# Fused attention and two-layer product on one core: norms a pair later, second products moved between batches, weights in four transfers

The chip is one Trainium2 chip, of which one core runs the kernel. The metric is device time in microseconds of that core, as the median of several executions. "Span" is the length of the one profiled execution of a kernel, 1.7 to 2.0 us less than the timed figure of that same execution. In the profiles PE is TensorE, the matrix engine (PEld its weight loads), DVE is VectorE, ACT is ScalarE, POOL is GpSimd, and SP issues most transfers; L129 is line 129 of that kernel (the lines of the two kernels differ). The granted clock is the share of its full clock that the profile shows TensorE as having been given.

## What the kernel computes

```python
# q, k, v: (8 batches, 12 heads, 448 rows, 64)   w_in: (768, 2048)   w_out: (2048, 768)
q_n = q / (norm(q) + 1e-6);  k_n = k / (norm(k) + 1e-6)
attn = softmax(q_n @ k_n.T / tau)                    # per head
x = (attn @ v) with heads side by side               # 3584 x 768
h = x @ w_in
out = (h * clip(h + 3, 0, 6) / 6) @ w_out            # float32
```

The kernel treats two heads at a time: six pairs make a batch, 48 pairs in all. Scores can't overflow (the inputs are unit vectors), so the exponential takes no maximum first. While the attention of one batch runs, the two products of an earlier batch are fed to TensorE piece by piece as filling: this is "the stream". A unit of the first product is 6 matmuls of 448 columns, followed by a relu on ACT and a multiplication on DVE; a unit of the second product is 16 matmuls of 384 columns, followed by one copy and an out transfer.

## The kernel before

Cuts are marked.

```python
def square(i, eng):                       # cut: eng None splits it over ACT and DVE (pair 0 only)
    sq = sb.tile([128, 2, 7, D], FP32, name="sq", tag="sq", bufs=2)
    eng.tensor_tensor(out=sq[:, :, :, :], in0=a, in1=a, op=ALU.mult)

def norms(i):
    nc.vector.tensor_reduce(out=n2[:, :], in_=sq..., axis=AX.X, op=ALU.add)      # L129, DVE
    nc.scalar.activation(out=ln[:, :], in_=n2[:, :], func=AF.Ln)                 # L132, ACT
    nc.scalar.activation(out=nr[:, :], in_=ln[:, :], func=AF.Exp, scale=0.5)
    nc.scalar.activation(out=le[:, :], in_=nr[:, :], func=AF.Ln, bias=eps_bias[:, :])
    nc.scalar.activation(out=r[:, :], in_=le[:, :], func=AF.Exp, scale=-1.0)     # L135

def add_batch(b):                         # called when batch b's attention is done
    first = [mm1_unit(b, fc) for fc in range(FCN)] if b < B else []
    second = []
    if b > 0:
        p = b - 1
        second = [mm2_unit(p, t, m) for t in range(3 + p % 2) for m in range(2)]
    # cut: appends first to the stream with second spread evenly between

for i in range(NP):                       # a pair; four steps s, each one group of scores
    for s in range(4):
        # cut: at the third step of a batch's first pair: add_batch(i // HP - 1)
        scores(i, s, SC2 if i < HP and s % 2 else SC)      # matmuls, then exponential on ACT
        if s == 0:
            # cut: every second pair issues the loads of a later group of two pairs
            if i + 3 < NP:
                square(i + 3, nc.gpsimd)
            if i + 2 < NP:
                normalise(i + 2, nc.gpsimd)
                vcast(i + 2, nc.gpsimd)
            next_weights()                                 # one of eight transfers
            fill(0.6 * ns)
            if i > 0:
                values(i - 1, 3)
                finish_values(i - 1)                       # reciprocal and scaling on DVE
            fill(0.4 * ns)
        elif s == 1:
            fill(0.8 * ns)
            if i > 0:
                back(i - 1)                                # transposes back, copy to xT on DVE
            if i + 3 < NP:
                norms(i + 3)
            fill(0.2 * ns)
        elif s == 2:
            fill(0.4 * ns)
            if i + 1 < NP:
                transposes(i + 1)
            fill(0.6 * ns)
            values(i, 0)
            values(i, 1)
        else:
            fill(ns)
            values(i, 2)
```

A `norms` call stands in ACT's queue between two exponentials, and in the traces everything behind it there waits as long as it waits: from pair 12 to pair 42 ACT stood 54.4 us in 30 waits, 1.8 us each, at the first instruction of `norms`, with the next exponential behind it.

## Time and profile before

| | before |
|---|---|
| timed median | 510.05 us |
| span of the profiled run | 509.7 us |
| first exponential starts | 17.39 us |
| mark of pair 5 (end of the first batch) | 52.33 us |
| length between marks of pairs 6 and 12 | 56.85 us |
| sum of the next five such stretches | 283.5 us |
| ACT idle until a DVE reduction | 86.8 us |

"Mark" means the start of the reciprocal that closes a pair on DVE; there is one per pair, so marks date the parts of a run. The lines these figures come from are in the prediction. The profiled execution was itself timed at 511.44 us, 1.4 above the median.

### The profile page before, as it was taken

What the parts mean: (1) busy time and instruction counts of PE and PEld (TensorE: products, weight loads), DVE (VectorE), ACT (ScalarE), POOL (GpSimd) and SP (SyncE); (2) the same over time, 40 slices, a digit from 0 to 9 for tenths busy, and PEclk for the clock granted to TensorE, in tenths of its full rate; (3) what the DMA queues carried; (4) which work ended last, traced back from release to release, by engine and by line L of the source; (5) the groups of instructions that cost most, each with busy time, mean ns of one, the idle gap of its engine ahead of it and who ended that gap; (6) DMA issues with size and microseconds to landing.
All of it is one profiled execution on the core that took longest, in us unless ns stands there. A gap on an engine that the chain in (4) does not pass through costs nothing.

```text
span 509.7 us, 9679 instructions
## 1 busy us (share of the span) xinstructions
PE 449.6 (88%) x3872; PEld 274.9 (54%) x3872; DVE 259.3 (51%) x568; ACT 282.5 (55%) x543; POOL 189.3 (37%) x156
## 2 busy tenths in 40 slices
PE   0666767779999999999999999999999999999996
PEld 0343434445555656655555656655555656655563
DVE  5665545554645555554645555545645454433310
ACT  3566646666566655566566655566565655533300
POOL 2996275444344343344354343344353320000000
PEclk9988989999999999999999999999999999999999
DMA  7999994210432504514432505514431000010022
GB/s 211 251 221 221 239 221 110 68 41 17 125 97 60 140 15 140 140 39 120 125 90 66 141 18 139 141 36 120 125 107 50 32 27 21 32 48 32 31 78 63
DMA packets 71581, 50.96 MB, mean 100 GB/s; under 512 B 22384, under 2 KB 71536, under 8 KB 71536
## 3 DMA queue, kind: packets, MB, share of 16 engines
q1 hardware_dynamic: 65168, 43.53, 31.5%
q0 software_dynamic: 5248, 6.29, 7.0%
q8 instruction: 30, 0.49, 0.4%
q10 hardware_dynamic: 1120, 0.52, 0.4%
q14 instruction: 15, 0.12, 0.1%
HBM read 45.61 MB, written 11.01 MB: 111 GB/s over the span
## 4 chain that ended last, share of the span: by engine, by line
PE 60%; ACT 15%; DVE 10%; DMA 7%; SPq 4%; issue 2%; POOL 1%; ACTq 0%; POOLq 0%
PE M L286 17%; PE M L257 13%; PE SC L184 9%; PE Y L286 8%; ACT at L188 7%; PE Y L257 7%; DVE n L129 6%; DMA raw<-in_q_dram 5%; PE PV L214 4%; ACT le L134 2%; DVE xT L241 2%; PE Z L240 2%; SPq L95 1%; ACT u L267 1%; ACT nr L133 1%
## 5 line engine op out<-in xcount | busy, mean ns | idle before, releaser
L188 ACT ACTIVATE at<-SC 128x896 bf16<-128x896 f32 x192 | 156.4, 820 | 65.2 <-PE SC L184 63.7
L141 POOL TENSOR_TENSOR nrm<-raw,r 128x896 bf16<-128x896 f32 x46 | 77.6, 1687 | 206.9 <-ACT r L135 196.5
L184 PE MATMUL SC<-qT,kz 128*128 128x448 bf16 x336 | 97.9, 363 | 29.7 <-ACT at L188 28.4
L257 PE MATMUL M<-xT,w_in_sb 128*128 128x448 bf16 x510 | 120.8, 353 | 0.0
L286 PE MATMUL M<-w_out_sb,gT 128*128 128x384 bf16 x608 | 118.1, 326 | 0.0
L286 PEld LDWEIGHTS <-gT 128*128 128x128 bf16 x896 | 84.5, 98 | 60.2 <-issue 5.2
L257 PEld LDWEIGHTS <-w_in_sb 128*128 128x128 bf16 x768 | 72.5, 98 | 77.3 <-issue 22.1
L270 DVE SCALAR_TENSOR_TENSOR gT<-u,M 128x448 bf16<-128x448 bf16 x85 | 52.7, 621 | 98.3 <-ACT u L267 97.9
L119 POOL TENSOR_TENSOR sq<-raw 128x896 f32<-128x896 f32 x46 | 77.3, 1680 | 18.7 <-DMA raw<-in_q_dram 12.2
L214 PEld LDWEIGHTS <-at 128*128 128x128 bf16 x1344 | 64.0, 99 | 30.8 <-ACT at L188 9.3
L214 PE MATMUL PV<-vx,at 128*128 128x65 bf16 (+1 forms) x1344 | 71.7, 199 | 7.0 <-ACT at L188 6.9
L267 ACT ACTIVATE u<-M,half_bias 128x448 bf16<-128x448 f32 x85 | 53.4, 630 | 22.6 <-PE M L257 22.3
L257 PE MATMUL Y<-xT,w_in_sb 128*128 128x448 bf16 x258 | 63.1, 355 | 0.0
L132 ACT ACTIVATE ln<-n 128x14 f32<-128x14 f32 x48 | 10.3, 215 | 86.8 <-DVE n L129 86.8
L286 PE MATMUL Y<-w_out_sb,gT 128*128 128x384 bf16 x288 | 56.7, 326 | 0.0
L129 DVE TENSOR_REDUCE n<-sq 128x14 f32<-128x896 f32 x48 | 51.6, 1076 | 6.7 <-POOL sq L119 4.5
L270 DVE SCALAR_TENSOR_TENSOR gT<-u,Y 128x448 bf16<-128x448 bf16 x43 | 26.7, 621 | 46.3 <-ACT u L267 45.9
L184 PEld LDWEIGHTS <-kz 128*128 128x128 bf16 x336 | 29.7, 99 | 21.3 <-issue 7.9
L154 PE MATMUL Z<-ident,nrm 128*128 128x128 bf16 x336 | 27.9, 225 | 13.4 <-DVE nrm L141 11.4
L154 PEld LDWEIGHTS <-nrm 128*128 128x128 bf16 x336 | 23.9, 101 | 23.5 <-DVE nrm L141 11.4
L229 DVE TENSOR_TENSOR on<-PV,rc 128x512 bf16<-128x512 f32 x48 | 33.2, 691 | 1.7
L241 DVE COPY xT<-Z 128x448 bf16<-128x448 bf16 x48 | 18.7, 389 | 29.1 <-PE Z L240 29.1
(44 smaller groups left out, 244.7 us busy)
## 6 DMA issues: line engine op xcount, KB each, us to landing
out_dram<-o SPq DMA_DIRECT2D x48, 192.0 KB, 1.9
raw<-in_q_dram SPq DMA_DIRECT2D x23, 384.0 KB, 5.1
raw<-in_k_dram SPq DMA_DIRECT2D x23, 384.0 KB, 5.2
vr<-in_v_dram SPq DMA_DIRECT2D x23, 384.0 KB, 5.5
w_in_sb<-in_moe_w_in_dram POOLq DMA_DIRECT2D x4, 768.0 KB, 11.7
w_out_sb<-in_moe_w_out_dram POOLq DMA_DIRECT2D x4, 768.0 KB, 12.2
out_dram<-o SPq DMA_DIRECT2D x16, 96.0 KB, 2.2
raw<-in_q_dram SPq DMA_DIRECT2D x23, 64.0 KB, 4.8
```

Source lines behind the costliest of these rows:

```text
L119: eng.tensor_tensor(out=sq[:, :, :, :], in0=a, in1=a, op=ALU.mult)
L129: nc.vector.tensor_reduce(out=n2[:, :], in_=sq[:, :, :, :].rearrange("p h s d -> p (h s) d"), axis=AX.X, op=ALU.add)
L141: eng.tensor_tensor(out=nrm[:, :, :, :].rearrange("p s h d -> p h s d"), in0=raw_pair(i), in1=r_of[i][:, :].rearrange("p (h s) -> p h s", ...
L154: nc.tensor.transpose(Z[:, s * 128 : (s + 1) * 128], nrm[:, s, :, :], ident[:, :])
L184: nc.tensor.matmul(sc[:, n, 0:S], k_block(i, name), qT_of[i][:, :], start=True, stop=True)
L188: nc.scalar.activation(out=at[:, 0:m, :], in_=sc[:, 0:m, 0:S], func=AF.Exp, scale=inv_tau)
L214: nc.tensor.matmul(o, at[:, n, q_cols(i // HP, j)], mv, start=(name == "A0" and j % 2 == 0), stop=last, skip_group_check=True,)
L229: nc.vector.tensor_tensor(out=on[:, :, :, :].rearrange("p (b j) h d -> p b (j h) d", b=2), in0=pv4[:, :, :, 0:D], in1=rc[:, :, :].to_broad ...
L257: nc.tensor.matmul(ps[:, 0:S], w_in_sb[:, cc, fc * 128 : (fc + 1) * 128], x[:, cc, c0 : c0 + S], start=(cc == 0), stop=(cc == CC - 1),)
L267: nc.scalar.activation(out=u[:, :], in_=ps[:, 0:S], func=AF.Relu, bias=half_bias[:, :], scale=1.0 / 6.0)
L270: nc.vector.scalar_tensor_tensor(out=g[:, fc, c0 : c0 + S], in0=u[:, :], scalar=1.0, in1=ps[:, 0:S], op0=ALU.min, op1=ALU.mult,)
L286: nc.tensor.matmul(ps[:, 0:MH], lhs, w_out_sb[:, fc, m * MH : (m + 1) * MH], start=(fc == 0), stop=(fc == FCN - 1),)
```

## The change

Its intent is to fill TensorE earlier and to keep other engines from holding it up. The core of the diff; renamings and the untouched parts of the moved functions are cut.

```diff
+    def square(i, n_act, eng):          # ACT squares the first n_act of 7 slices, eng the rest
+    def reduce(i):                      # the DVE reduction, taken out of norms
...
     def add_batch(b):
-        second = [mm2_unit(p, t, m) ...]      # of the batch before, p = b - 1
+        first = [mm1_unit(b, fc) for fc in range(FCN)]
+        for n, u in enumerate(first):
+            stream.append(u)
+            if lagging and n % 3 == 2:
+                stream.append(lagging.pop(0))
+        second = [mm2_unit(b, t, m) for t in range(3 + b % 2) for m in range(2)]
+        n = len(second) - (LAG if 0 < b < B - 1 else 0)      # LAG = 4
+        stream.extend(second[:n])
+        lagging.extend(second[n:])
...
-    nc.scalar.preload_act_table_set(...)      # the second one
-    load(1); load(2)
+    load_qk(1); load_v(0); load_qk(2); load_v(1); load_v(2)
...      # eight weight transfers become four, at the start and at pairs 0, 3 and 5
-    square(0, None); norms(0); square(1, nc.vector); normalise(0, nc.vector); vcast(0, nc.gpsimd)
-    norms(1); transposes(0); normalise(1, nc.vector); square(2, nc.gpsimd); vcast(1, nc.gpsimd)
-    next_weights(); norms(2)
+    square(0, 3, nc.vector); reduce(0); norms(0); square(1, 4, nc.gpsimd); reduce(1)
+    normalise(0, nc.vector); transposes(0); norms(1); vcast(0, nc.gpsimd)
+    square(2, 4, nc.gpsimd); normalise(1, nc.gpsimd); vcast(1, nc.gpsimd)
+    next_weights(); reduce(2)
...
             if s == 0:
-                square(i + 3, nc.gpsimd); normalise(i + 2, nc.gpsimd); vcast(i + 2, nc.gpsimd)
             elif s == 1:
+                norms(i + 2)
                 fill(0.8 * ns)
                 back(i - 1)
-                norms(i + 3)
             elif s == 2:
+                square(i + 3, 3 if i < HP else 0, nc.gpsimd)
+                normalise(i + 2, nc.gpsimd); vcast(i + 2, nc.gpsimd)
             else:
+                reduce(i + 3)
```

More of the change, by code (lines that the diff above doesn't have):

```diff
@@ L74, with load_qk @@
     moe_banks = [Y]
-    raw_of, nrm_of, r_of, qT_of, at_of, on_of = {}, {}, {}, {}, {}, {}
-    def load(d, n_pairs=2, first=0, engs=None):
+    raw_of, sq_of, n2_of, nrm_of, r_of, qT_of, at_of, on_of = {}, {}, {}, {}, {}, {}, {}, {}
+    def load_qk(d, first=0, n_pairs=2, e0=nc.sync, e1=nc.sync):
         b, h = 2 * d // HP, 4 * d % H + 2 * first
@@ L84, in load @@
         raw = raw_of[d][:, 2 * first : 2 * (first + n_pairs), :, :]
-        vt = vr[d % NV][:, 2 * first : 2 * (first + n_pairs), :, :]
         hs = slice(h, h + 2 * n_pairs)
-        e0, e1 = engs or (nc.sync, nc.sync)
-        def main(t):
-            return t[b, hs, 0:SM, :].rearrange("h (p c) d -> p h c d", c=3)
         for n, t in enumerate((k, q) if b % 2 else (q, k)):
-            e0.dma_start(out=raw[:, :, 4 * n : 4 * n + 3, :], in_=main(t))
+            e0.dma_start(
+                out=raw[:, :, 4 * n : 4 * n + 3, :],
+                in_=t[b, hs, 0:SM, :].rearrange("h (p c) d -> p h c d", c=3),
+            )
             e1.dma_start(
@@ L98, in load, with load_v @@
             )
-        e1.dma_start(out=vt[:, :, 0:3, :], in_=main(v))
+    def load_v(d):
+        b, h = 2 * d // HP, 4 * d % H
+        vt, vs = vr[d % NV], v[b, h : h + 4]
+        nc.sync.dma_start(
+            out=vt[:, :, 0:3, :], in_=vs[:, 0:SM, :].rearrange("h (p c) d -> p h c d", c=3)
+        )
         for g in range(2):
-            e0.dma_start(
-                out=vt[64 * g : 64 * g + 64, :, 3, :].rearrange("p (i g) d -> p i g d", g=2)[:, :, g, :],
-                in_=v[b, hs, SM:S, :].rearrange("(i g) p d -> p i g d", g=2)[:, :, g, :],
+            nc.sync.dma_start(
+                out=vt[64 * g : 64 * g + 64, g:4:2, 3, :],
+                in_=vs[g:4:2, SM:S, :].rearrange("h p d -> p h d"),
             )
@@ L107, in raw_pair @@
         return raw_of[i // 2][:, 2 * (i % 2) : 2 * (i % 2) + 2, :, :]
-    def square(i, eng):
+    def square(i, n_act, eng):
         sq = sb.tile([128, 2, 7, D], FP32, name="sq", tag="sq", bufs=2)
-        r_of[i] = sq
+        sq_of[i] = sq
         a = raw_pair(i)
-        if eng is None:
-            nc.scalar.activation(out=sq[:, :, 0:3, :], in_=a[:, :, 0:3, :], func=AF.Square)
-            nc.vector.tensor_tensor(
-                out=sq[:, :, 3:7, :], in0=a[:, :, 3:7, :], in1=a[:, :, 3:7, :], op=ALU.mult
-            )
-        else:
-            eng.tensor_tensor(out=sq[:, :, :, :], in0=a, in1=a, op=ALU.mult)
+        if n_act:
+            nc.scalar.activation(
+                out=sq[:, :, 0:n_act, :], in_=a[:, :, 0:n_act, :], func=AF.Square
+            )
+        if n_act < 7:
+            eng.tensor_tensor(
+                out=sq[:, :, n_act:7, :], in0=a[:, :, n_act:7, :], in1=a[:, :, n_act:7, :], op=ALU.mult
+            )
+    def reduce(i):
+        n2 = sb.tile([128, 14], FP32, name="n2", tag="n2", bufs=3)
+        n2_of[i] = n2
+        nc.vector.tensor_reduce(
+            out=n2[:, :],
+            in_=sq_of.pop(i)[:, :, :, :].rearrange("p h s d -> p (h s) d"),
+            axis=AX.X,
+            op=ALU.add,
+        )
     def norms(i):
-        sq = r_of[i]
-        n2 = sb.tile([128, 14], FP32, name="n2", tag="n2", bufs=2)
+        n2 = n2_of.pop(i)
         ln = sb.tile([128, 14], FP32, name="ln", tag="ln", bufs=2)
@@ L128, in norms @@
         r = sb.tile([128, 14], FP32, name="r", tag="r", bufs=3)
-        nc.vector.tensor_reduce(
-            out=n2[:, :], in_=sq[:, :, :, :].rearrange("p h s d -> p (h s) d"), axis=AX.X, op=ALU.add
-        )
         nc.scalar.activation(out=ln[:, :], in_=n2[:, :], func=AF.Ln)
@@ L321, in fill @@
             stream_ns[0] -= step
+    LAG = 4
+    lagging = []
     def add_batch(b):
-        first = [mm1_unit(b, fc) for fc in range(FCN)] if b < B else []
-        second = []
-        if b > 0:
-            p = b - 1
-            second = [mm2_unit(p, t, m) for t in range(3 + p % 2) for m in range(2)]
-        stream_ns[0] += len(first) * CC * MM1_NS + len(second) * FCN * MM2_NS
-        done = 0
+        first = [mm1_unit(b, fc) for fc in range(FCN)]
         for n, u in enumerate(first):
             stream.append(u)
-            while second and done * len(first) < (n + 1) * (6 + 2 * ((b - 1) % 2)) - len(first):
-                stream.append(second.pop(0))
-                done += 1
-        stream.extend(second)
+            if lagging and n % 3 == 2:
+                stream.append(lagging.pop(0))
+                stream_ns[0] += FCN * MM2_NS
+        second = [mm2_unit(b, t, m) for t in range(3 + b % 2) for m in range(2)]
+        n = len(second) - (LAG if 0 < b < B - 1 else 0)
+        stream.extend(second[:n])
+        lagging.extend(second[n:])
+        stream_ns[0] += FCN * CC * MM1_NS + n * FCN * MM2_NS
     for t in vr:
@@ L342 @@
         nc.vector.memset(t[0:64, 1:4:2, 3, :], 0.0)
-    load(0, 1, 0, (nc.sync, nc.scalar))
-    load(0, 1, 1, (nc.sync, nc.scalar))
-    nc.scalar.preload_act_table_set("natural_log_exp_and_others")
-    load(1)
-    load(2)
+    load_qk(0, 0, 1, nc.sync, nc.scalar)
+    load_qk(0, 1, 1, nc.sync, nc.scalar)
+    load_qk(1)
+    load_v(0)
+    load_qk(2)
+    load_v(1)
+    load_v(2)
     nc.vector.memset(eps_bias, EPS)
@@ L350 @@
     make_identity(nc, ident)
-    nc.gpsimd.memset(kz[0][:, :, :], 0.0)
     for t in vx:
@@ L356 @@
         nc.vector.memset(t[64:128, 1, 3, D : D + 1], 1.0)
-    nc.gpsimd.memset(kz[1][:, :, :], 0.0)
-    FG = d_ff // 4
-    weights = [
-        (w_in_sb[:, :, f * FG : (f + 1) * FG], w_in_r[:, :, f * FG : (f + 1) * FG]) for f in range(4)
-    ] + [(w_out_sb[:, 4 * f : 4 * f + 4, :], w_out_r[:, 4 * f : 4 * f + 4, :]) for f in range(4)]
+    for t in kz:
+        nc.gpsimd.memset(t[:, :, :], 0.0)
+    weights = []
+    for f in range(2):
+        c = slice(f * d_ff // 2, (f + 1) * d_ff // 2)
+        weights.append((w_in_sb[:, :, c], w_in_r[:, :, c]))
+    for f in range(2):
+        c = slice(f * FCN // 2, (f + 1) * FCN // 2)
+        weights.append((w_out_sb[:, c, :], w_out_r[:, c, :]))
     def next_weights():
-        if weights:
-            o, w = weights.pop(0)
-            nc.gpsimd.dma_start(out=o, in_=w)
-    square(0, None)
+        o, w = weights.pop(0)
+        nc.gpsimd.dma_start(out=o, in_=w)
+    square(0, 3, nc.vector)
+    reduce(0)
     norms(0)
-    square(1, nc.vector)
+    square(1, 4, nc.gpsimd)
+    reduce(1)
     normalise(0, nc.vector)
+    transposes(0)
+    norms(1)
     vcast(0, nc.gpsimd)
-    norms(1)
-    transposes(0)
-    normalise(1, nc.vector)
-    square(2, nc.gpsimd)
+    square(2, 4, nc.gpsimd)
+    normalise(1, nc.gpsimd)
     vcast(1, nc.gpsimd)
     next_weights()
-    norms(2)
+    reduce(2)
     startup = ExitStack()
@@ L405 @@
                 if i % 2 and (i + 5) // 2 < NP // 2:
-                    load((i + 5) // 2)
-                if i + 3 < NP:
-                    square(i + 3, nc.gpsimd)
-                if i + 2 < NP:
-                    normalise(i + 2, nc.gpsimd)
-                    vcast(i + 2, nc.gpsimd)
-                next_weights()
+                    load_qk((i + 5) // 2)
+                    load_v((i + 5) // 2)
                 fill(0.6 * ns)
@@ L418 @@
             elif s == 1:
+                if i + 2 < NP:
+                    norms(i + 2)
                 fill(0.8 * ns)
@@ L421 @@
                     back(i - 1)
-                if i + 3 < NP:
-                    norms(i + 3)
                 fill(0.2 * ns)
             elif s == 2:
+                if i + 3 < NP:
+                    square(i + 3, 3 if i < HP else 0, nc.gpsimd)
+                if i + 2 < NP:
+                    normalise(i + 2, nc.gpsimd)
+                    vcast(i + 2, nc.gpsimd)
+                if i in (0, 3, 5):
+                    next_weights()
                 fill(0.4 * ns)
@@ L432 @@
             else:
+                if i + 3 < NP:
+                    reduce(i + 3)
                 fill(ns)
@@ L440 @@
     add_batch(B - 1)
-    add_batch(B)
     fill(1e9)
```

## The prediction

> **What bounds the kernel now.** I read the page's busy table and slices first, then stretches of time cut at the batches of heads, then who waits for whom, then the start instruction by instruction.
>
> ```profile
> PE   0666767779999999999999999999999999999996
> DMA  7999994210432504514432505514431000010022
> L129 DVE TENSOR_REDUCE n<-sq 128x14 f32<-128x896 f32 x48 | 51.6, 1076 | 6.7 <-POOL sq L119 4.5
> ```
>
> A digit is 12.7 us. From slice 9 on (115 us) TensorE is at 9; before that it is at 6 or 7, and there the DMA engines are at 9. So there are two regimes: a front of some 115 us where TensorE idles, and a long part where it is nearly full. To date the parts I use the reciprocal that closes each pair of heads (one per pair, 48 in all):
>
> ```profile
> 52.33 0.21 DVE L228 RECIPROCAL rc<-PV 128x8 f32<-128x8 f32 x1 [1.87 <-PE PV L214]
> 61.13 0.20 DVE L228 RECIPROCAL rc<-PV 128x8 f32<-128x8 f32 x1
> 72.84 0.20 DVE L228 RECIPROCAL rc<-PV 128x8 f32<-128x8 f32 x1
> 117.98 0.20 DVE L228 RECIPROCAL rc<-PV 128x8 f32<-128x8 f32 x1
> ```
>
> These are pairs 5, 6, 7 and 12; pair 0's is at 22.56. So the first batch (no streamed product yet) ran at (52.33 - 22.56)/5 = 5.95 us a pair. The stretches between pairs 6, 12, 18, 24, 30, 36 and 42:
>
> ```profile
> 61.13:117.98 56.85, 41.89 (x383) 24.46 (x382) 29.82 (x67) 32.92 (x66) 28.75 (x22) 0.97 0.44 109
> 117.98:172.50 54.52, 52.05 (x468) 32.19 (x467) 31.39 (x69) 34.44 (x67) 23.29 (x18) 1.00 0.32 89
> 172.50:232.33 59.83, 57.59 (x504) 35.86 (x503) 31.68 (x68) 35.11 (x68) 23.28 (x18) 1.00 0.35 97
> ```
>
> Columns: length, then busy us (instructions) of PE, PEld, DVE, ACT, POOL, then granted clock, DMA share, GB/s. The second batch's stretch holds 41.89 us of TensorE work in 56.85 us: 15.0 us idle. The later stretches are 95 to 96% busy; the five from 117.98 to 401.46 lose 12.1 us together. Their waits:
>
> ```profile
> PE SC L184 <- ACT at L188: 12.0, 23, 0.8
> ACT ln L132 <- DVE n L129: 54.4, 30, 2.0
> ```
>
> All 12.1 us of TensorE idleness there is scores waiting for an exponential, and in the chain of waits nearly every such place is preceded by a DVE reduction and the four norm instructions on ACT. ScalarE is in order: it stands about 1.8 us per pair in front of the norms until DVE has reduced, and the exponential queues behind. The worst instance in the front:
>
> ```profile
> 63.64 1.67 POOL L119 TENSOR_TENSOR sq<-raw 128x896 f32<-128x896 f32 x1 [8.02 <-DMA raw<-in_q_dram]
> 65.34 1.09 DVE L129 TENSOR_REDUCE n<-sq 128x14 f32<-128x896 f32 x1 [2.28 <-POOL sq L119]
> 66.46 0.21 ACT L132 ACTIVATE ln<-n 128x14 f32<-128x14 f32 x1 [4.36 <-DVE n L129]
> 68.42 0.35 PE L184 MATMUL SC<-qT,kz 128*128 128x448 bf16 x1 [3.40 <-ACT at L188]
> ```
>
> A load landing at 63.6 stops POOL, DVE, ACT and PE in turn, for a pair whose scores are three pairs away.
>
> **Budget.** TensorE is busy 449.6 us; 0.9 before 13 us and 25.4 between 13.3 and 52.33, so 423.3 us lie after 52.33. The span's remainder is 509.7 - 52.33 = 457.4, so 34.1 us are not busy: 15.0 (second batch), 12.1 (five full stretches), 4.4 (from the last matmul's end near 505.3 to the end), about 2.6 elsewhere. All streamed work lies after pair 5's mark before and after the change, and its amount does not change. So end = mark + 423.3 + idle, and I need the new mark and the new idle time.
>
> **What the Trainium skill says.**
> - "TensorE: Matmul & The Clock Gate", Wait — 56ns, not 53.3ns?: warm start-to-start is N/2.4 GHz + 2.5 ns, so 162.5 ns for 384 columns. The trace agrees: 16 second-product matmuls advance the chain by 2.60 us. A unit of the second product costs 2.6 us, one of the first (6 x 190 ns) 1.14.
> - "DMA: Bandwidth & Descriptors", Issuing engines are not separate DMA queues: transfers from all issuers share 16 engines. The trace agrees: the weights, issued by POOL from 15.8 to 54.8 us, share saturated slices with the head loads, whose issue on SP then takes up to 5.5 us instead of 0.6. Moving them between issues adds no bandwidth.
> - "GPSIMD Engine Reference", 4.1 Engine selection: two-input elementwise work is about 2x slower on GPSIMD. Here 1.68 us for a square on POOL against 1.08 on DVE: 1.55x, so partly agreed.
>
> **The change, part by part.**
> 1. *Start.* ScalarE now has six DMA issues and a second table load (6.25 to 7.53) before its first square at 7.54. Two issues and that load go, so the square can start when the data lands, near 5.1. DVE's first reduction starts at 8.10 now; I expect about 5.8. But the second pair's reduction is put ahead of the first normalise on DVE and waits for ACT squares queued behind the first norms, so the first transposes gain only some 0.5 us (11.45 to about 11). The larger gain is behind them: ACT now does three pairs' norms before its first exponential (17.39, though scores were ready at about 14). The third pair's norms move behind the second exponential. Scores at about 12.7 give the first exponential at 13.5 to 14.5. Call it 3 us earlier.
> 2. *First batch.* POOL per pair now: 1.68 square + 1.69 normalise + 0.63 cast + 0.9 weight issue = 4.9, in series with reduce, norms and exponentials. The change puts 3/7 of the square on ACT (0.52, from the one such instruction in the trace) and leaves POOL 4/7 of 1.68 = 0.96, and the norms no longer wait. ACT then has 3 x 0.91 + 0.54 + 1.05 (norms end to end, 9.22 to 10.27) + 0.52 = 4.85 us and becomes the limit; with small gaps 5.1. Five pairs save 5 x 0.85 = 4.2. Together with 1, the mark goes from 52.33 to about 45.2.
> 3. *Norms a pair later.* Reduction at the fourth step, norms at the second step of the next pair. POOL runs ahead, so the reduction should be ready and the 54.4 us of ACT waits vanish. ACT's load is 63% in the full stretches (34.44/54.52), so I expect most of the 12.1 us of idle to go: 5 left.
> 4. *Stream.* Stretch by stretch the streamed work is now 18.2, 33.8, 39, 33.8, 39, 33.8, 39 and a tail of 54.7 us (16 first-product units, then 6 or 8 second-product units of the previous batch). It becomes 33.8, 28.6, 33.8, 39, 33.8, 39, 33.8 and 49.5: 15.6 us move into the second batch, which has 15.0 idle, 10.4 leave full stretches and 5.2 the tail. By itself this only pays for as much idle as it fills.
> 5. *Load stall.* The square that stopped for 8.02 us is issued half a pair later, and the norms behind it a whole pair later. Loads landing at 45.3 and 63.6 are bound by the saturated transfers; the four bigger weight transfers have half as many packets for the first weight, worth perhaps 2 us. With the mark 7 us earlier, I keep 2 to 3 us of stall. Parts 4 and 5 leave second-batch idle of about 5 (2.5 load stall, 2.5 ScalarE queueing) in place of 15.0.
>
> Sum: 45.2 + 423.3 + 5 + 5 + 4.4 + 2 = 484.9 us. The timed median is 0.9 above the profile's span now; I keep 485.
>
> **Rivals.**
> - *The loads set the front.* For: DMA slices at 9 up to 72 us, squares that waited for landings. Against: first-batch landings only stopped POOL twice (4.2 and 6.4 us). If true, the earlier mark turns into waits in pairs 5 to 9, losing about 6 us: 491.
> - *ScalarE becomes the limit.* The second batch now runs 16 first-product units in a row: per pair 3.28 exponentials + 1.05 norms + 5 x 0.63 relu = 7.5 us in a pair of about 8.7. The score buffer is single from the second batch on, so each exponential delayed by a relu stops scores. If 0.3 us a pair is lost over 42 pairs, 12.6 us come back: about 497. Against: before, such waits hardly occurred except behind norms.
> - *The norms were not the cause of the 12 us.* Then it stays near 12: 492. For: only 23 waits, short. Against: the chain passes through the reduction before nearly all of them.
>
> **Range and chances.** The optimistic end is no load stall and 2 us idle in the full part: about 478. One rival in full gives 491 to 497, the loads plus uncaused norms about 498. Two per cent faster is 500.4. I take 477 to 494, and 95% for faster, since three separate gains (7 us of mark, 10 in the second batch, 7 behind norms) would have to fail for most of their worth.
>
> **What would show it.** Right: pair 5's reciprocal near 45; first exponential before 15; ACT's wait for the reduction far under 87 us; TensorE idle of some 5 us in the second batch's stretch; full stretches at 98% or more; PE's busy sum near 450. Wrong: the mark staying near 50 with POOL or ACT waiting for head loads; scores still waiting 10 us or more for exponentials with relus ahead of them; a slower clock from new gaps; or out transfers holding up loads on SP in the second batch.

## The result

The changed kernel takes 484.29 us (483.17 to 488.87, four runs) against 510.05 for the kernel before (509.06 to 512.22). The ratio is 0.9506, with a 95% interval of 0.9435 to 0.9578. Ratios here are the mean time of one kernel's runs over that of the kernel before in the same rounds, so not quite the quotient of the medians. A repeat beside other kernels gave 484.76 us and 0.9527. The prediction was 485.

The profile after, the same views. First the slices of the page, each now 12.0 us long:

```profile
PE   0757989999899999999999999999989999999995
DMA  7999991256105541552351523531541000000012
```

TensorE is at 9 from the seventh slice on (72 us, with two slices at 8 later), rather than from 115 us. The DMA engines still run at 9 through the front. Next the marks of pairs 5, 6, 7 and 12:

```profile
46.99 0.21 DVE L239 RECIPROCAL rc<-PV 128x8 f32<-128x8 f32 x1
57.29 0.20 DVE L239 RECIPROCAL rc<-PV 128x8 f32<-128x8 f32 x1
67.29 0.20 DVE L239 RECIPROCAL rc<-PV 128x8 f32<-128x8 f32 x1
111.54 0.20 DVE L239 RECIPROCAL rc<-PV 128x8 f32<-128x8 f32 x1
```

The first exponential starts at 13.79 and pair 0's mark is at 19.02. Then the stretches from pair 6 on (columns as in the prediction):

```profile
57.29:111.54 54.25, 51.58 (x468) 32.00 (x467) 31.28 (x68) 34.77 (x68) 24.95 (x19) 1.00 0.55 141
111.54:161.73 50.19, 47.50 (x441) 29.39 (x440) 31.06 (x67) 34.17 (x66) 23.32 (x18) 1.00 0.39 103
161.73:213.89 52.16, 51.17 (x468) 31.85 (x467) 31.71 (x68) 35.21 (x67) 23.32 (x18) 1.00 0.38 102
```

The second batch's stretch is hardly shorter than before, but it now holds 468 matmul records in place of 383 and leaves 2.7 us idle in place of 15.0. And TensorE's waits in the five stretches from 111.54 to 383.83:

```profile
PE Z L165 <- DVE xT L252: 7.3, 11, 1.0
PE Z L251 <- DVE on L240: 0.5, 2, 0.3
```

No score waits for an exponential there any more, where before it was 12.0 us. The wait that took its place is new in rank: the next pair's transposes wait until DVE has emptied the bank `Z` that the back-transposes had filled. Over the whole run ACT waits 5.8 us for a reduction, in place of 86.8 (total us, times, longest):

```profile
ACT ln L143 <- DVE n L129: 5.8, 3, 2.7
```

### The profile page after: what moved, and what is told of

It reads as the page before. It is cut to its first block, busy times and chain, and to the rows that moved or that the text cites. A ratio compares the mean times of both kernels' runs of the same rounds, so it can differ in the third digit from the quotient of the medians.

```text
span 481.2 us, 9709 instructions
## 1 busy us (share of the span) xinstructions
PE 443.3 (92%) x3872; PEld 272.5 (57%) x3872; DVE 259.2 (54%) x566; ACT 287.8 (60%) x550; POOL 183.5 (38%) x154
## 4 chain that ended last, share of the span: by engine, by line
PE 75%; DMA 9%; ACT 7%; SPq 4%; DVE 3%; issue 1%; POOL 0%; ACTq 0%; POOLq 0%
PE M L297 20%; PE M L268 15%; PE SC L195 10%; PE Y L297 10%; PE PV L225 8%; PE Y L268 8%; DMA vr<-in_v_dram 5%; DMA raw<-in_q_dram 4%; PE Z L165 4%; ACT at L199 3%; ACT u L278 2%; DVE gT L281 2%; PE Z L251 1%; SPq L104 1%; SPq L88 1%; SPq L92 1%
## 5 line engine op out<-in xcount | busy, mean ns | idle before, releaser
L152 POOL TENSOR_TENSOR nrm<-raw,r 128x896 bf16<-128x896 f32 x47 | 79.4, 1690 | 193.1 <-ACT r L146 178.8
L297 PE MATMUL M<-w_out_sb,gT 128*128 128x384 bf16 x592 | 115.0, 326 | 0.0
L195 PE MATMUL SC<-qT,kz 128*128 128x448 bf16 x336 | 96.6, 359 | 1.8 <-ACT at L199 0.9
L122 POOL TENSOR_TENSOR sq<-raw 128x896 f32<-128x896 f32 (+2 forms) x47 | 73.5, 1564 | 23.3 <-DVE gT L281 10.2
L268 PE MATMUL Y<-xT,w_in_sb 128*128 128x448 bf16 x252 | 61.3, 352 | 0.0
L297 PE MATMUL Y<-w_out_sb,gT 128*128 128x384 bf16 x304 | 59.9, 326 | 0.0
L278 ACT ACTIVATE u<-Y,half_bias 128x448 bf16<-128x448 f32 x42 | 26.5, 631 | 15.7 <-PE Y L268 15.4
L160 POOL CAST vx<-vr 128x512 bf16<-128x512 f32 x48 | 29.4, 613 | 5.4 <-DMA vr<-in_v_dram 5.4
```

What stands on the lines that cost most here:

```text
L122: eng.tensor_tensor(out=sq[:, :, n_act:7, :], in0=a[:, :, n_act:7, :], in1=a[:, :, n_act:7, :], op=ALU.mult)
L152: eng.tensor_tensor(out=nrm[:, :, :, :].rearrange("p s h d -> p h s d"), in0=raw_pair(i), in1=r_of[i][:, :].rearrange("p (h s) -> p h s", ...
L195: nc.tensor.matmul(sc[:, n, 0:S], k_block(i, name), qT_of[i][:, :], start=True, stop=True)
L268: nc.tensor.matmul(ps[:, 0:S], w_in_sb[:, cc, fc * 128 : (fc + 1) * 128], x[:, cc, c0 : c0 + S], start=(cc == 0), stop=(cc == CC - 1),)
L278: nc.scalar.activation(out=u[:, :], in_=ps[:, 0:S], func=AF.Relu, bias=half_bias[:, :], scale=1.0 / 6.0)
L297: nc.tensor.matmul(ps[:, 0:MH], lhs, w_out_sb[:, fc, m * MH : (m + 1) * MH], start=(fc == 0), stop=(fc == FCN - 1),)
```

## Experiments

All ran to correct results. Edits are against the changed kernel unless said otherwise.

### 1. The stream alone

Edit, on the kernel before: only `add_batch` is replaced by the new one.

> The kernel before with the new order of the streamed products alone. Theory (the front has idle TensorE time because of two stalls, the load landing near 63.6 us and the norms ahead of exponentials; the shift only fills the part of it that queued TensorE work can use): of the 15.0 us idle in the second batch's stretch 6 to 9 go, the full stretches keep their 12 us of waits for exponentials, the mark of pair 5 stays at 52.3; so about 502 us (ratio 0.98). Rival (the shift is the change's main gain, it alone takes the 15.6 us off the end): about 494 (0.97 or less). Third (the stalls bind the stretch whatever is queued): within 2 us of before.

Measured: 504.79 us, 0.9901 (0.9881 to 0.9921). Mark of pair 5 at 52.16. The second batch's stretch:

```profile
63.04:119.59 56.55, 52.06 (x468) 32.22 (x467) 31.00 (x68) 34.67 (x68) 28.75 (x22) 1.00 0.42 114
```

Its idle time falls from 15.0 to 4.5 us, nearly as in the changed kernel. Yet only 5.7 us come off the end, because part of it is lost again elsewhere: from pair 12 to 42 TensorE is now idle for 16.9 us in place of 12.1 (15.7 of it in waits for exponentials, which the theory had expected to stay at 12), and from pair 5 to 6 the run takes 10.88 us in place of 8.80. The rival, that the shift alone brings 15.6 us, falls; the theory's 502 was 3 us too hopeful.

### 2. Everything but the stream

Edit: `add_batch` and its calls as in the kernel before.

> The changed kernel with the old order of the streamed products (all second-product units wait for the next batch). Theory: the mark stays at 47, the full stretches keep idle of about 1 to 2 us each, and the second batch, with 42 us of TensorE work, ends sooner than 57 us but is held by the load landing near 63 us and by ACT (about 6.1 us a pair); it loses 5 to 9 us of TensorE time, so about 490 (0.961), some 6 us slower than the change. Rival (the stream is the main gain): 497 or more. If the earlier norms and the stream were worth the same idle time twice, it would be within 2 us of the change.

Measured: 490.83 us, 0.9621 (0.9561 to 0.9680), so 6.1 us slower by the medians than the changed kernel in the same rounds. The second batch's stretch again runs short of work:

```profile
55.05:109.38 54.33, 41.03 (x383) 24.40 (x382) 30.25 (x66) 33.81 (x65) 24.90 (x19) 0.97 0.55 138
```

It leaves 13.3 us idle. In it POOL waits 11.2 us for a q to land, until 64.31. The stream is worth some 6 us, whether it is added first or last; that is much less than the work it moves, because with the old order the same stretch would simply have held less work. The second of the two measures is weak by itself, since the intervals overlap (the repeat of the changed kernel in these rounds has 0.9465 to 0.9588); the first, run 1, is clear of noise.

### 3. Norms back in their old places

```diff
             if s == 0:
+                square(i + 3, 3 if i < HP else 0, nc.gpsimd)
+                normalise(i + 2, nc.gpsimd); vcast(i + 2, nc.gpsimd)
             elif s == 1:
-                norms(i + 2)
                 fill(0.8 * ns)
                 back(i - 1)
+                reduce(i + 3); norms(i + 3)
             elif s == 2:
-                square(...); normalise(i + 2, ...); vcast(i + 2, ...)
             else:
-                reduce(i + 3)
```

and `norms(2)` before the loop, as before.

> The changed kernel with square, normalise and cast back at the first step of a pair, and reduction with norms of the third-next pair back behind the back-transposes, as in the kernel before; loads, weights, stream and the split of the square stay changed. Theory: ACT again stands some 1 to 2 us a pair before the norms, scores wait for exponentials in the full stretches for about 12 us in place of none, the load landing near 63 us stops ACT again, and the first exponential is late again: 10 to 16 us slower than the change, 494 to 500 (0.97 to 0.98). Rival (waits of scores for exponentials come from the single score buffer, not from the norms): full stretches stay at under 2 us idle each and the time within 5 us of the change.

Measured: 505.42 us, 0.9920 (0.9888 to 0.9952): 20.7 us slower than the changed kernel in the same rounds, more than the 10 to 16 expected. The waits from pair 12 to pair 42 (119.96 to 404.77):

```profile
ACT ln L143 <- DVE n L129: 55.3, 30, 2.0
PE SC L195 <- ACT at L199: 15.4, 26, 1.2
```

and two of its stretches, which hold the same number of matmul records as those of the changed kernel shown above:

```profile
119.96:173.12 53.16, 48.41 (x441) 29.70 (x440) 30.25 (x68) 33.98 (x67) 23.31 (x18) 1.00 0.36 96
173.12:228.00 54.88, 52.12 (x468) 32.08 (x467) 31.10 (x69) 34.67 (x67) 23.31 (x18) 1.00 0.36 95
```

53.16 against 50.19 us for 441 records, 54.88 against 52.16 for 468. Over the five stretches it is 284.8 against 272.3 us: 12.5 us. The mark of pair 5 is at 52.69 (5.7 us later), and the rest lies in the second batch (2.7 us) and behind pair 42 (1.2 us). So the place of the norms, with that of the squares, reductions and normalises that go with them, is the largest part of the change, both in the front and in the full part. This run moves them together; their shares were not separated, though the wait of 55.3 us that returns is the one before the norms. The rival, that the single score buffer caused the waits, falls: with the same buffer and the norms elsewhere there are none.

The full stretches cost about what was expected (12.5 us); the expectation had put too little on the other parts. Only 8.8 of these 12.5 us are idle time, though. For 468 records TensorE is "busy" 52.12 us here and 51.17 us in the changed kernel. The record of a `values` matmul lasts 199 ns while the next one starts 30 ns after it; in a train the records overlap, and at each wait the last record's tail stands alone and counts as busy. Reading the starts of the matmuls in the trace bears this out: in 173.12:228.00 there are five waits, all but one us of their 3.7 us of delay counts as idle, and the remaining 1.0 us is five tails. (The profile models the ends of matmul records; the starts are measured.)

### 4. The norms' places alone

Edit: old stream, eight weight transfers, old order of loads, squares of the first batch on POOL alone. What stays is the place of squares, reductions, norms and normalises, and the start's new order of them.

> The changed kernel with everything undone but the places of square, reduction, norms and normalise (and the start's order of them): old stream, eight weight transfers, old order of loads, squares of the first batch on POOL alone. Theory (the stream is worth 6 us as its own undoing and its own doing both showed, loads, weights and the split nothing): within 2 us of the run without the new stream, 489 to 493 (0.962). Rival (the split on ACT shortened the first batch): mark of pair 5 at 50 or later and 494 or more.

Measured: 490.71 us, 0.9593 (0.9549 to 0.9636), like run 2. So in the presence of the new norms (and of the new order of the start, which no run tests by itself), the loads' order, the number of weight transfers and the split of the square are worth nothing together that shows. In their absence the same: run 3, which has these and the stream, is at 0.9920, and the stream alone at 0.9901. Pair 5's mark is at 51.80 here, later than in run 2 (47.32), but little of that reaches the end: the second batch's stretch is 49.42 us long in place of 54.33.

### 5. Loads and weights one at a time

Order of the first loads as before:

```diff
-    load_qk(1); load_v(0); load_qk(2); load_v(1); load_v(2)
+    load_v(0); load_qk(1); load_v(1); load_qk(2); load_v(2)
```

> The changed kernel with each load of v straight behind its q and k, as before, in the first three loads. Theory: the second pair group's q and k land 1.5 to 2.5 us later (0.46 MB of v ahead of them at some 215 GB/s), which delays the ACT square of pair 2 that stands before the first exponential: first exponential about 2 us later than 13.79, mark of pair 5 up to 2 us later than 46.99, unless the load landings near 33.8 us hide it, as saturated transfers would: 484 to 486. Rival (the order is worth nothing, since the total transferred by the time that counts is the same): under 0.5 us.

Measured: 483.78 us, 0.9485 (0.9461 to 0.9508). Not slower than the changed kernel. The theory's first half (a start 2 us later) falls: the first exponential starts at 14.05, 0.3 us later. In its profile the mark is 3.6 us later, at 50.56, after POOL had waited 8.8 us for a q to land, and the mark of pair 12 is 2 us later; but this execution was the slowest of the four (485.16).

Eight weight transfers:

```diff
-                if i in (0, 3, 5):
+                if weights:
                     next_weights()
```

with the list of eight.

> The changed kernel with the weights in eight transfers, the first where it was and one at the third step of each of the first seven pairs. Theory (the DMA engines are saturated until some 60 us and the bytes are the same, so size and number of weight transfers move little): within 2 us of the change. Smaller packets for the first weight cost at most 2 us in the front: 484 to 486. But the weights then arrive more evenly, so the pair-3 stall on a head load (5.84 us on POOL near 33.8 us) may shrink by 1 to 2 us. Rival (four large transfers are a real gain by fewer descriptors on POOL and fewer packets): 488 or more.

Measured: 484.33 us, 0.9514 (0.9467 to 0.9561): the same. One of its four runs, the profiled one, took 488.57 us; there the mark is at 52.12, after POOL had waited 11.5 us for a q to land. Single runs of the changed kernel scatter likewise, from 483.1 to 490.3 us.

### 6. Weights issued later

The scatter, and the front of the changed kernel, point at landings. Pair 3 is stopped by one (the lines are POOL, DVE and PE, with the idle time before them in brackets):

```profile
33.78 1.04 POOL L122 TENSOR_TENSOR sq<-raw 128x512 f32<-128x512 f32 x1 [5.84 <-DMA raw<-in_q_dram]
34.85 1.09 DVE L129 TENSOR_REDUCE n<-sq 128x14 f32<-128x896 f32 x1 [2.65 <-POOL sq L122]
36.96 0.40 PE L251 MATMUL Z<-ident,on 128*128 128x128 bf16 x4 [3.86 <-DVE on L240]
```

Half of the weights had been issued by 21 us, though the first product starts at 49 us and the second at 80 us.

```diff
-    vcast(1, nc.gpsimd)
-    next_weights()
+    vcast(1, nc.gpsimd)
...
-                if i in (0, 3, 5):
+                if i in (0, 3, 6, 7):
                     next_weights()
```

> The changed kernel with the four weight transfers issued later, at pairs 0, 3, 6 and 7 in place of the start and pairs 0, 3 and 5, so that head loads of the front share the DMA engines with less. Theory (the front is bound by landings: POOL waited 5.84 us for q at 33.8 and the square at 63.5 stood 10.2 us): pair 3's stall of some 2.6 us goes and the landing near 63.4 comes earlier, the mark falls to about 44, time 480 to 482, if no first or second product waits for its weights. Rival (ACT sets the first batch's pace and landings only cost what they cost by chance): within 1 us of the change. Counter-effect: products waiting for late weights, visible as matmuls waiting on a weight DMA, 487 or more.

Measured: 477.30 us (476.79 to 477.62), 0.9360 (0.9341 to 0.9380): better than expected, and without the scatter. The front of the changed kernel and of this one, from the start to pair 5's mark:

```profile
0.00:46.99 46.99, 25.22 (x283) 15.78 (x283) 27.66 (x78) 31.94 (x67) 27.76 (x33) 0.96 1.03 233
```

```profile
0.00:43.32 43.32, 24.38 (x281) 14.76 (x282) 27.64 (x78) 31.79 (x67) 28.64 (x34) 1.00 1.01 233
```

The DMA engines are as full and move as much, but the right bytes come first; the mark falls by 3.7 us, and TensorE's clock is granted in full. More is lost than the stop itself: from pair 5 to pair 6, with the same 74 matmul records, the changed kernel and then this one show

```profile
46.99:57.29 10.30, 9.62 (x74) 5.60 (x73) 5.22 (x11) 6.31 (x12) 5.88 (x6) 0.83 1.15 235
```

```profile
43.32:52.34 9.02, 8.36 (x74) 4.87 (x74) 5.22 (x11) 6.20 (x13) 5.82 (x5) 1.00 1.14 268
```

at a granted clock of 0.83 and 1.00. In the changed kernel it was 0.69 in the pair right behind the stop, and with eight transfers, after the stop of 11.5 us, 0.70 from pair 5 to 6. What lowers the clock was not tested. No matmul waits for weights. So the landings did set the front, as the first rival of the prediction said, though it named pairs 5 to 9 and the damage was at pair 3. Number and size of the weight transfers did nothing that could be measured; their time did. In the profiles the gain is 5.4 us (475.8 against 481.2); by the medians it is 7, since the slow executions are gone too.

### 7. The share of ACT in the squares

On the late-weights kernel, where no landing hides it:

```diff
-                    square(i + 3, 3 if i < HP else 0, nc.gpsimd)
+                    square(i + 3, 0, nc.gpsimd)
```

> The late-weights kernel with the whole square of the first batch on POOL (no share on ACT). In the late-weights run the marks of pairs 0 and 5 are 19.24 and 43.32, 4.82 us a pair, and ACT is without gaps there. Theory (ACT sets that pace): without its 0.52 us square ACT needs 4.3 us a pair, POOL 1.68 + 1.69 + 0.61 = 4.0, so the mark falls by up to 2.5 us to about 41 and the time to about 475 (0.931). Rival (POOL would set the pace, the split was what made the first batch faster): mark 45 or later, 479 or more. Third (loads landing set the mark): no change within 0.5 us.

Measured: 477.46 us, 0.9332 (0.9291 to 0.9373); mark at 42.84 after a first mark at 18.86, so 4.80 us a pair against 4.82. From pair 0's mark to pair 5's, the late-weights kernel and then this one:

```profile
19.24:43.32 24.08, 17.21 (x230) 10.43 (x229) 17.58 (x40) 22.60 (x46) 18.75 (x19) 1.00 1.10 232
```

```profile
18.86:42.84 23.98, 16.70 (x228) 10.47 (x229) 17.59 (x41) 20.15 (x41) 22.88 (x20) 1.00 1.11 236
```

ACT loses 2.45 us of work, POOL gains 4.1, and the length stays. ACT was 94% busy, but it isn't the bound: relieved, it waits for scores instead. Nor did POOL take its place at the same pace: it is 95% busy now, but no engine waits for it in this stretch.

```profile
ACT at L199 <- PE SC L195: 3.1, 6, 0.5
PE Z L251 <- DVE on L240: 6.3, 5, 1.3
```

These are this run's waits in the same stretch. The second line comes once per pair in both kernels: the back-transposes stand in TensorE's queue before the third scores, and wait for DVE's reciprocal and scaling of the pair before. This loop over TensorE, DVE and ACT is the candidate for the pace of 4.8 us; it was not tested by taking it away. That the split of the square is worth nothing is shown.

### 8. No lag

```diff
-    LAG = 4
+    LAG = 0
```

> The changed kernel with LAG at 0: every batch's second product comes right behind its own first product, nothing lags into the next batch. Same TensorE work, 10.4 us of it moves from the tail and from other stretches. Theory (TensorE is full from the second batch on, so only idle time counts, and ACT at 65% keeps up): within 2 us of the change, 482 to 486. Rival (the lagging units are there to spread the relu work, since a first product in one piece needs 5 relu per pair on ACT): score waits for exponentials, or first-product matmuls waiting for their evictions, come back for 1 us or more per batch, 6 us or more in all: 490 and over.

Measured: 487.64 us, 0.9587 (0.9529 to 0.9644); 3 us over the changed kernel, between the two expectations, and the intervals overlap. Its profile is 3.7 us longer from pair 6's mark to the end (429.0 against 425.3 us in the repeat of the changed kernel). The wait that grows is that of the transposes for DVE's copy: 14.2 us over the run against 9.6. So the lag is worth at most a little; that it works by spreading DVE's and ACT's work on first-product units is not shown. Scores do not wait for exponentials here either (1.2 us in all).

### 9. The repeat of the changed kernel

> The changed kernel once more, on the same chip as the three others, as their measure: 484 us, ratio 0.950 within 0.007.

Measured: 484.76 us (483.13 to 490.27), 0.9527 (0.9465 to 0.9588). Span 481.7, stretches like the first profile's within 0.1 us from pair 12 on, the front within 1 us.

### 10. Later transposes: the best version

On the late-weights kernel, the wait that replaced the old one is taken away by putting streamed work ahead of it:

```diff
             elif s == 2:
-                fill(0.4 * ns)
+                fill(0.8 * ns)
                 if i + 1 < NP:
                     transposes(i + 1)
-                fill(0.6 * ns)
+                fill(0.2 * ns)
```

> The late-weights kernel with the transposes of the next pair after 0.8 instead of 0.4 of the third step's streamed work. In the full stretches the only TensorE wait left is these transposes waiting for the DVE copy that empties the same bank: 9.6 us in 14 cases. Theory (0.6 us more work ahead of them covers it): the 9.6 us go nearly all, stretches without idle, about 469 (0.919). Rival (the copies behind the transposes then come too late for the next pair's scores, or DVE queues): the waits move to scores, time within 2 us of 477.

Measured: 469.84 us (469.46 to 470.52), 0.9186 (0.9146 to 0.9226). Of the waits of transposes for the copy, 9.6 us in the run, 2.1 are left:

```profile
PE Z L165 <- DVE xT L252: 2.1, 8, 0.6
```

and one of the full stretches:

```profile
205.08:262.11 57.03, 57.03 (x505) 35.79 (x504) 32.01 (x68) 35.17 (x68) 23.29 (x18) 1.00 0.36 101
```

57.03 us for 505 records without a gap, where the changed kernel takes 58.89 for 504:

```profile
213.89:272.78 58.89, 57.27 (x504) 35.70 (x503) 31.86 (x69) 35.13 (x69) 23.31 (x18) 1.00 0.35 99
```

The next pair's scores do not come late.

With the square on POOL as well:

> Both edits of the two runs before on the late-weights kernel. If each works as its theory says and they touch different stretches: 466 to 468 (0.914). If one fails, the other one's time.

Measured: 470.22 us, 0.9194 (0.9147 to 0.9242): the other edit's time, as run 7 lets one expect. The late-weights kernel itself ran in other rounds on another chip; against run 7, in the same rounds as these two (477.46), the later transposes are worth 7.2 us. Run 10's kernel is the best version found, 8% below the kernel before and 3% below the changed one.

## Why the prediction was right

The time was right (485 against 484.29), and the sum had the right form, but so close a hit is partly luck. The sum is one of a profiled span, and there it was 3.7 us too high, with terms off in opposite directions. From span to time the prediction added next to nothing (0.1), while the median came out 3.1 above the span, since the four executions spread from 483.2 to 488.9, a spread that is gone in run 6. In terms of the profiled span:

| term | predicted | measured |
|---|---|---|
| mark of pair 5 | 45.2 | 46.99 |
| TensorE busy after the mark | 423.3 | 443.3 - 25.2 = 418.1 |
| idle in the second batch | 5 | 0.7 + 2.7 = 3.4 |
| idle in the five full stretches | 5 | 7.9 |
| tail | 4.4 | 4.9 |
| elsewhere | 2 | 0.0 |
| sum | 484.9 | 481.2 |

The two idle terms are near their forecast for another reason than the one given. The prediction kept 2.5 us of load stall and 2.5 of ScalarE queueing in the second batch, and scores waiting for exponentials in the full stretches; what stands there is transposes waiting for DVE's copy, 2.3 of the 3.4 and 7.3 of the 7.9 us. Two of its signs did not come true: PE's busy sum is 443.3 and not near 450, and the five full stretches are 97.1% busy and not 98%.

*Start.* Right. First transposes at 11.09 (about 11), first reduction at 6.15 (5.8), first exponential at 13.79 (13.5 to 14.5); pair 0's mark 3.5 us earlier (3). The square starts at 4.00, as soon as its first load has landed.

*First batch.* The pace was better than predicted where nothing disturbed it (4.78 us a pair against 5.1), but pair 3 took 7.4 us because of a landing and the two pairs behind it 5.5 each, so the mean was 5.59. The reason given, that ACT becomes the limit and POOL's relief matters, was wrong: run 7 shows that the split changes nothing.

*Norms.* The mechanism was right and the main one: run 3 shows it, run 4 shows that it does most by itself (4.1% of the 4.9%). The size was wrong. The step that failed is the sentence that all streamed work lies behind the mark "and its amount does not change", taken as TensorE's busy time. The work is the same, the busy time is not: it fell by 5.2 us, from 423.3 to 418.1. Behind the mark both traces hold 3591 matmul records, with 47 idle gaps before and 20 after; 27 gaps fewer, each with a tail of 0.17 us, make 4.6 us as an estimate. One page of the Trainium skill gives the reason to be wary: the page "Trainium Kernel Development and Optimization", Performance Expectations, calls matmul busy time "a bad metric" for nearness to the roofline because matmuls are pipelined. The trace agrees that busy time misleads here (52.12 us in run 3 and 51.17 us in the changed kernel for the same 468 records). The term of the full stretches, 12.1 us of idle of which 5 were to be left, should have compared lengths at equal counts of records, and comes to 12.5 saved.

*Stream.* The caution was right: it pays only for the idle time that it fills. It is worth some 6 us. The 2 us allowed for fewer packets per weight transfer did not show (run 5: eight transfers, the same time).

*Load stall and rivals.* The stall near 63 us stayed on POOL (the square starts at 63.51, before it was 63.64) but hardly reaches TensorE any more (0.3 us). The rival that loads set the front was half true; run 6 shows that 7 us lay there to be had. The rival of ACT as the limit did not occur: no scores wait for exponentials in the full stretches. The third rival is refuted by run 3. What nobody had listed is the wait that took the old one's place, transposes behind DVE's copy, which run 10 removes.

## What to carry to other kernels

An instruction that waits in an in-order queue costs what stands behind it; giving its input half an iteration more of lead (the norms came a whole pair later, what feeds them half a pair) was worth 20 us here, while moving 15.6 us of matmuls into an idle stretch was worth 6. When the transfer engines are full, ask which bytes are needed first, not how many transfers carry them. And judge a full matrix engine by the length of stretches with equal instruction counts, not by its busy time; then look for the next wait in rank, since one usually steps up.

## What the Trainium skill lacked or had wrong

- "Trainium Kernel Development and Optimization" (Performance Expectations) warns of matmul busy time but gives no size: the same 468 matmuls were busy 52.12 us with waits in between and 51.17 us with fewer.
- "DMA: Bandwidth & Descriptors" (Issuing engines are not separate DMA queues) says that issuers share the engines, but not that the time of issue then decides: four weight transfers issued later gave 477.30 us in place of some 484, at nearly the same DMA share up to pair 5's mark (1.01 and 1.03). Its advice (Bandwidth, Measured) to batch transfers to 1 MiB and more brought no gain in time here, where other loads shared the engines: eight transfers of 768 KB, 484.33 us; four of 1536 KB, 484.29 and 484.76 us. The moments of issue differed too, and no run measures the bandwidth of one such transfer alone.
- "GPSIMD Engine Reference" (4.1 Engine selection) has GPSIMD about 2x slower than VectorE on two-input work; for 896 float32 elements per partition it is 1.55x here (1.68 against 1.08 us).
- No page that was read says that an engine at 94% busy in a stretch may still not bound it: taking 2.45 us off ACT left the stretch from pair 0 to pair 5 at 24.0 us (24.08 before).
